# Gated product written in token order, one store per output tile, and idle products between the first groups

## The chip, the cores and the metric

The kernel runs on one core of a Trainium2 chip. The metric is the device time of one execution in microseconds. The core has a matrix engine (TensorE, in the profile PE for products and PEld for weight loads), VectorE (DVE), ScalarE (ACT), GpSimd (POOL), and SyncE (SP), which issues most of the DMA transfers. Sixteen DMA engines move the data.

## The reference

Attention over 8 batches, 12 heads, 448 tokens and head size 64, followed by a gated feed-forward layer with a product over the tokens. All inputs and the output are float32.

```python
q_n, k_n = rmsnorm(q, g_q), rmsnorm(k, g_k)
attn = softmax(q_n @ k_n.T / 8)
x = concat_heads(attn @ v)                     # 8 x 448 x 768
h = relu(x @ w_in)                             # 8 x 448 x 1024
u, v = h[..., :512], h[..., 512:]
v_n = (v - mean(v)) / sqrt(var(v) + 1e-6)
v_s = einsum('ts,bsd->btd', w_spatial, v_n) + b_spatial[None, :, None]
out = (u * v_s) @ w_out                        # 8 x 448 x 768
```

## The kernel before, in words

The order of all work is written out by hand in one string, PLAN: some 1,600 words, each of the form name.arguments/slots/engine. A word `S.3.1/12` calls `op_S` for group 3 and unit 1 with the PSUM banks 1 and 2; a last field a, v or g puts the work on ScalarE, VectorE or GpSimd. The words are run through once when the program is built, so each engine gets its instructions in the order in which its words stand, and each engine carries them out in that order. Waits between engines follow from the tiles that are read and written. PSUM is one tile `ps` of 8 banks of 512 float32 columns; the plan says which bank each result takes.

Attention goes by 24 groups (a batch and four of its heads). A group's q, k and v are loaded into `raw` (op_L, lines 287 and 292), squared (Q, L379 and L381), summed (R, L392), turned into a factor 1/rms (I and J, L405 and L410), multiplied (N, L425) and transposed, in the first groups by TensorE (P, L444, copied out by K, L362 and L463), later by a DMA transpose (T, L480). Scores are 64 x 32 products (S, L505), exponentials are taken by ScalarE (E, L513), and sums and weighted values come from TensorE again (s, a and b, L538). X (L567) divides and writes `xt`.

A token t of 448 is held as t = 7 p + c, with p below 64 and c below 7: partition p loads seven tokens that lie side by side in memory. From there on the columns of `xt` stand in the order c, p: column 64 c + p.

The second part goes by batch. V (L583, and L612 for the last 64 rows) and U (L649) multiply by the two halves of `w_in`, c and u apply the relu, B, M, m and A normalise, H (L663) is the product with `w_spT` over tokens, G (L668, VectorE) multiplies the result in PSUM by `us` and writes the gated product `gt`, and O (L677, L612 for the last rows) multiplies `gt`, as 128-column weights, by `w_out`. The 448 tokens make three tiles of 128 rows and one of 64. The copies out of PSUM (o, L360 and L362) fill `os`, and t stores it. Because the rows stand in the order c, p, a 128-row tile m holds the tokens with c = 2m in its first 64 rows and those with c = 2m + 1 in its last, and each half goes out by a transfer of its own (L701), 64 rows of 768 values that lie seven tokens apart in memory. The half tile of 64 rows goes out by L698, in the last batch in two pieces of 384 columns. All stores are issued by SyncE, as are the loads and the DMA transposes.

The words z (op_z, L252) are products of the identity with itself whose result nobody reads; they stand at the start and between the first groups. Y (L347) transposes `w_sp` by TensorE, reading its weights seven elements apart. `w_sp` lies in the space of `gt`, and so has the name gt in the profile.

Of the kernel before, what the change touches and what calls it, by code (L numbers as in the profile page):

```python
# [12 lines left out]
ALU = mybir.AluOpType  # L13
# [14 lines left out]
E.0.4/4/a P.1.0/4 R.2.1 L.6.0/2 Q.4.0/0/g E.0.3/5/a P.1.1/5 K.1.0/1/v I.2//a z.5/2 J.2//a K.1.1/1/v Q.3.0/1/a wi.1.3
N.2.1/2/v S.1.1/23 E.0.6/6/a wx//g S.1.2/45 S.1.0/67 N.2.0/3/v E.1.2/7/a L.1.2/5 P.2.1/0 E.1.0/8/a R.4.0 S.1.3/45
Q.3.1/2/g L.6.1/4 P.2.0/1 E.1.1/9/a K.2.1/2/v S.1.5/67 E.1.3/a/a R.3.0 S.1.6/23 Q.4.1/0/g Y.2/0 E.1.5/b/a K.2.0/2/v  # L30
R.3.1 E.1.6/c/a S.1.4/45 S.2.6/67 Q.5.0/1/g Y.0/1 E.2.6/d/a R.4.1 I.3//a S.2.3/23 s.0.3.1/67 J.3//a wi.1.0 s.0.1.1
E.1.4/e/a F.0//v s.0.2.1 s.0.0.1 y.0//v s.0.6.1 L.5.1/3 s.0.5.1 N.3.0/0/g E.2.3/f/a R.5.0 S.2.5/45 s.0.4.1 Y.1/1
I.4//a D.0/1/a E.2.5/g/a N.3.1/1/v L.7.1/8 P.3.0/6 D.1/0/a S.2.4/23 K.3.0/3/v L.2.2/7 S.2.1/45 F.1//g P.3.1/7
Q.6.1/2/a y.2//v y.1//v Q.6.0/0/g L.3.2/5 a.0.2.1/06 E.2.4/h/a K.3.1/3/v a.0.5.1 a.0.4.1 a.0.1.1 R.6.1 E.2.1/i/a
S.3.1/12 b.0.2.1/37 b.0.0.1 wi.0.2 b.0.6.1 E.3.1/j/a Q.5.1/1/v a.0.6.1 b.0.4.1 wi.1.2 S.3.0/45 a.0.3.1 d.0//a S.3.6/12
wi.1.1 a.0.0.1 J.4//a b.0.1.1 E.3.6/k/a N.4.1/2/v b.0.5.1 wi.0.0 b.0.3.1 E.3.0/l/a S.3.4/12 X.0.0 L.8.1/1 N.4.0/3/g
E.3.4/7/a R.5.1 S.3.3/45 E.3.3/6/a Y.3/0 X.0.1 wi.0.3 F.2//v d.1//a S.3.5/12 S.2.0/34 wi.0.1 I.5//a P.4.0/5 X.1.0
E.2.0/c/a F.3//g X.1.1 P.4.1/6 J.5//a E.3.5/e/a K.4.0/0/v N.5.1/0/g S.3.2/34 K.4.1/0/v s.2.3.1/57 E.3.2/8/a S.2.2/12
s.2.1.1 y.3//v s.2.6.1 s.2.5.1 a.2.3.1/06 E.2.2/1/a s.2.0.1 N.5.0/1/v T.5.1/0 s.2.4.1 a.2.1.1 b.2.5.1/34 Q.7.0/2/a
S.4.4/12 s.2.2.1 R.6.0 b.2.3.1 Q.7.1/1/g a.2.6.1 T.5.0/1 E.4.4/5/a b.2.0.1 a.2.0.1 b.2.1.1 R.7.0 a.2.5.1 I.6//a  # L40
a.2.4.1 D.2/1/a b.2.2.1 L.5.2/6 b.2.4.1 Q.8.1/0/g a.2.2.1 D.3/0/a R.7.1 b.2.6.1 S.4.6/12 d.2//a z.1/5 V.0.1.0/5
E.4.6/9/a L.4.2/7 X.2.0 V.0.0.0/7 L.9.1/5 X.2.1 I.7//a V.0.0.1 d.3//a L.8.0/3 Z.5/1/v V.0.1.1 J.7//a J.6//a L.9.0/9
X.3.1 S.4.1/01 N.6.1/3/g S.4.5/23 X.3.0 E.4.1/0/a V.0.1.2 V.0.2.0/4 c.0.1//v E.4.5/3/a V.0.0.2 N.7.0/2/g R.8.1
L.10.1/4 S.5.5/01 c.0.0//a S.5.4/56 S.4.2/23 E.5.5/b/a V.0.2.2 V.0.2.1 E.4.2/2/a N.6.0/0/g U.0.2.1/7 c.0.2//v P.6.1/0
E.5.4/4/a B.0.1 U.0.2.2 S.5.3/12 N.7.1/1/g B.0.0 T.6.0/3 S.5.0/34 E.5.3/a/a W.0/5 K.6.1/3/v E.5.0/f/a B.0.2 T.7.0/2
F.4//g S.5.1/01 U.0.2.0 c.0.3//v E.5.1/6/a Q.8.0/2/g U.0.0.0/6 L.6.2/0 u.0.2//v S.5.2/23 S.4.3/45 T.7.1/1 B.0.3
S.4.0/01 E.5.2/c/a U.0.1.2/7 U.0.1.0 Q.9.0/1/g E.4.3/l/a U.0.0.2 L.11.1/2 U.0.0.1 L.10.0/8 M.0//a U.0.1.1 E.4.0/i/a
u.0.0//v L.11.0/7 S.6.3/23 F.5//g S.5.6/45 R.8.0 E.6.3/j/a U.0.3.0/6 U.0.3.1 Q.9.1/0/g L.15.1/6 U.0.3.2 E.5.6/g/a
u.0.1//v S.6.6/01 u.0.3//v s.4.3.1/23 m.0//a s.4.2.1 I.8//a s.4.5.1 E.6.6/e/a R.9.0 s.4.1.1 wo b.4.0.1/45 S.6.4/67
s.4.6.1 J.8//a s.4.0.1 E.6.4/h/a A.0.0 s.4.4.1 b.4.5.1 Z.7/2/v b.4.4.1 b.4.6.1 A.0.3 D.4/1/a a.4.4.1/01 A.0.1 b.4.2.1  # L50
D.5/0/a S.7.6/67 A.0.2 b.4.1.1 a.4.6.1 E.7.6/7/a R.9.1 a.4.2.1 N.8.1/3/g a.4.1.1 b.4.3.1 a.4.0.1 d.5//a a.4.5.1
S.7.0/23 d.4//a a.4.3.1 X.5.1 H.0.2/6 I.9//a Q.11.1/2/g E.7.0/1/a X.4.1 T.8.1/0 H.0.3/5 X.5.0 J.9//a Q.11.0/1/a G.0.2
H.0.0/7 L.7.2/1 N.9.0/0/g X.4.0 F.6//a S.7.5/12 R.11.0 S.7.4/34 H.0.1/0 Q.10.1/0/a L.12.0/0 G.0.0 V.1.1.0/6 Q.10.0/1/g
L.13.0/9 E.7.5/8/a G.0.1 V.1.1.2 V.1.0.0/7 G.0.3 E.7.4/d/a V.1.1.1 R.11.1 N.8.0/2/g V.1.0.2 c.1.1//a S.6.5/01 S.7.3/23
R.10.0 S.7.2/45 E.6.5/k/a V.1.0.1 Q.15.1/2/g O.0.0.1/6 T.8.0/0 R.10.1 E.7.2/5/a O.0.2.1/0 E.7.3/4/a O.0.0.0/1 L.12.1/3
o.0.2.1/0/v N.9.1/1/g I.11//a I.10//a o.0.0.1/1/v S.6.1/23 o.0.0.0//a W.1/504 c.1.0//v E.6.1/9/a t.0.0 B.1.1 F.7//g
Q.12.0/1/a S.6.0/67 o.0.3.1/2/v S.6.2/12 T.9.1/1 V.1.2.1/3 o.0.3.0//v E.6.2/g/a O.0.1.1/4 Z.8/0/v c.1.3//v J.11//a
t.0.3 J.10//a V.1.2.0 o.0.1.1/3/a N.10.0/3/g U.1.3.0/0 R.12.0 L.8.2/5 E.6.0/2/a V.1.2.2 T.9.0/1 S.7.1/12 B.1.3
c.1.2//a S.8.0/45 S.8.5/67 N.10.1/2/g E.7.1/c/a U.1.3.1 B.1.0 L.13.1/1 U.1.0.2/3 E.8.5/0/a U.1.0.0 B.1.2 U.1.0.1
U.1.3.2 Q.12.1/0/a N.11.0/1/g T.10.1/0 O.0.2.0/1 u.1.3//a R.12.1 U.1.2.1/2 E.8.0/6/a U.1.1.1/6 L.10.2/8 U.1.2.2  # L60
L.15.0/4 Z.9/1/v M.1//a U.1.2.0 I.12//a u.1.0//v m.1//a L.14.1/7 U.1.1.2 u.1.2//a A.1.3 s.6.5.1/07 o.0.2.0//a S.9.1/34
# [93 lines left out]
def kernel(  # L155
# [18 lines left out]
    C = 7  # L174
# [566 lines left out]
```

## Time and profile before

| | |
|---|---|
| median of 3 runs | 282.5 us (281.66 to 426.04) |
| profiled execution | 280.25 us |
| its span, first to last instruction | 278.3 us |
| TensorE busy | 257.6 us, 93% of the span |
| ScalarE busy | 217.3 us, 78% |
| VectorE busy | 211.6 us, 76% |
| GpSimd busy | 128.8 us, 46% |
| moved by DMA | 55.72 MB, mean 200 GB/s |
| stores of output tiles | 55 of 192 KB and 2 of 96 KB |

The profile cuts the span into 40 slices and gives each a digit, the busy share in tenths. A row of an engine's timeline gives the start, the length, the line, the operation, the tiles, and in brackets how long the engine had been idle and what released it. A row of a group gives the busy time of all its instructions and the mean of one in ns, and then the idle time ahead of them. The row PEclk is the clock that TensorE was granted. In a row of windows the DMA share can exceed 1, because the transfers' packets overlap.

### The profile page before, as it was taken

What the parts mean: (1) busy time and instruction counts of PE and PEld (TensorE: products, weight loads), DVE (VectorE), ACT (ScalarE), POOL (GpSimd) and SP (SyncE); (2) the same over time, 40 slices, a digit from 0 to 9 for tenths busy, and PEclk for the clock granted to TensorE, in tenths of its full rate; (3) what the DMA queues carried; (4) which work ended last, traced back from release to release, by engine and by line L of the source; (5) the groups of instructions that cost most, each with busy time, mean ns of one, the idle gap of its engine ahead of it and who ended that gap; (6) DMA issues with size and microseconds to landing.
All of it is one profiled execution on the core that took longest, in us unless ns stands there. A gap on an engine that the chain in (4) does not pass through costs nothing.

```text
span 278.3 us, 10091 instructions
## 1 busy us (share of the span) xinstructions
PE 257.6 (93%) x4322; PEld 129.8 (47%) x4322; DVE 211.6 (76%) x365; ACT 217.3 (78%) x359; POOL 128.8 (46%) x99
## 2 busy tenths in 40 slices
PE   7977988988898999979999989999999999999991
PEld 3535555434354454435535443455445545555550
DVE  3899799788788787879898877798868455657740
ACT  5598799979798998599999886999999977402531
POOL 2568877896875782863779566530021100000000
PEclk9997799999999999999999999999999999999999
DMA  6999899999999999999999999395946402260446
GB/s 197 320 364 252 219 227 171 300 224 337 198 292 194 303 191 299 167 240 316 200 251 248 237 251 291 75 217 110 210 134 147 103 6 55 69 178 13 105 115 179
DMA packets 59335, 55.72 MB, mean 200 GB/s; under 512 B 35865, under 2 KB 54938, under 8 KB 59290
## 3 DMA queue, kind: packets, MB, share of 16 engines
q1 hardware_dynamic: 57778, 52.31, 78.1%
q0 software_dynamic: 1504, 2.76, 5.5%
q8 instruction: 34, 0.56, 0.9%
q14 instruction: 11, 0.09, 0.1%
q10 hardware_dynamic: 8, 0.00, 0.0%
HBM read 38.55 MB, written 11.01 MB: 178 GB/s over the span
## 4 chain that ended last, share of the span: by engine, by line
PE 59%; DMA 12%; ACT 8%; issue 6%; POOL 6%; DVE 4%; SPq 2%; POOLq 0%; ACTq 0%; DVEq 0%
PE ps L538 11%; PE ps L677 10%; PE ps L649 9%; DMA raw<-in_k_dram 8%; PE ps L505 8%; PE ps L663 8%; PE ps L583 6%; ACT et L513 6%; POOL nrm L425 4%; DMA qT<-nrm 4%; PE ps L252 3%; PE ps L612 2%; DVE ss L392 2%; DVE nrm L425 1%; POOL sqt L381 1%
## 5 line engine op out<-in xcount | busy, mean ns | idle before, releaser
L513 ACT ACTIVATE et<-ps 128x896 bf16<-128x896 f32 x168 | 146.1, 919 | 17.1 <-PE ps L505 16.1
L381 POOL TENSOR_TENSOR sqt<-raw 128x896 f32<-128x896 f32 (+1 forms) x32 | 52.8, 1654 | 29.0 <-DVE nrm L425 10.8
L505 PE MATMUL ps<-qT,kT 64*32 64x448 bf16 x1344 | 57.7, 358 | 3.7 <-DMA qT<-nrm 1.8
L425 POOL TENSOR_TENSOR nrm<-raw,rs 128x896 bf16<-128x896 f32 x30 | 50.3, 1687 | 20.2 <-ACT rs L410 10.2
L392 DVE TENSOR_REDUCE ss<-sqt 128x14 f32<-128x896 f32 x46 | 48.9, 1076 | 4.1 <-ACT sqt L379 3.5
L649 PE MATMUL ps<-xt,w_in 128*128 128x448 bf16 x192 | 43.5, 353 | 1.8 <-ACT os L360 1.8
L538 PE MATMUL ps<-et,vt 64*32 64x448 bf16 x1344 | 41.6, 349 | 2.6 <-issue 2.5
L583 PE MATMUL ps<-w_in,xt 128*128 128x512 bf16 x144 | 36.6, 380 | 0.6 <-ACT et L513 0.6
L677 PE MATMUL ps<-w_out,gt 128*128 128x384 bf16 x192 | 36.1, 326 | 0.1
L567 DVE TENSOR_TENSOR xt<-ps,rc 128x448 bf16<-128x448 f32 x48 | 27.8, 617 | 10.4 <-PE ps L538 6.6
L505 PEld LDWEIGHTS <-kT 64*32 64x32 bf16 x1344 | 19.3, 90 | 32.0 <-issue 19.9
L315 POOL CAST vt<-raw 128x896 bf16<-128x896 f32 x18 | 16.7, 930 | 34.6 <-DMA raw<-in_v_dram 28.6
L663 PE MATMUL ps<-w_spT,vn 128*128 128x448 bf16 (+1 forms) x128 | 27.3, 353 | 1.7 <-issue 1.7
L649 PEld LDWEIGHTS <-w_in 128*128 128x128 bf16 x192 | 17.5, 98 | 21.5 <-issue 7.0
L538 PEld LDWEIGHTS <-vt 64*32 64x32 bf16 x1344 | 19.9, 93 | 15.6 <-issue 4.9
L624 DVE BATCH_NORM_STATS2 s<-vs 128x6 f32<-128x512 bf16 (+1 forms) x32 | 21.7, 679 | 6.4 <-ACT vs L574 6.1
L677 PEld LDWEIGHTS <-gt 128*128 128x128 bf16 x192 | 17.9, 98 | 16.0 <-issue 3.8
L360 ACT ACTIVATE os<-ps 128x384 f32<-128x384 f32 (+1 forms) x35 | 17.2, 490 | 8.9 <-PE ps L677 8.2
L538 PE MATMUL ps<-et,ones 64*32 64x448 bf16 x672 | 23.7, 368 | 0.2 <-DVE qT L362 0.2
L362 DVE COPY os<-ps 128x384 f32<-128x384 f32 (+1 forms) x29 | 15.7, 554 | 9.3 <-PE ps L677 7.2
L668 DVE TENSOR_TENSOR gt<-ps,us 128x448 bf16<-128x448 f32 x32 | 18.9, 617 | 3.5 <-PE ps L663 2.6
L583 PEld LDWEIGHTS <-xt 128*128 128x128 bf16 x144 | 12.9, 97 | 18.0 <-issue 5.9
(62 smaller groups left out, 269.8 us busy)
## 6 DMA issues: line engine op xcount, KB each, us to landing
out_dram<-os SPq DMA_DIRECT2D x55, 192.0 KB, 3.1
raw<-in_k_dram SPq DMA_DIRECT2D x23, 448.0 KB, 6.3
raw<-in_q_dram SPq DMA_DIRECT2D x23, 448.0 KB, 7.0
raw<-in_v_dram SPq DMA_DIRECT2D x12, 448.0 KB, 5.4
raw<-in_v_dram SPq DMA_DIRECT2D x24, 224.0 KB, 5.4
w_in<-in_moe_w_in_dram POOLq DMA_DIRECT2D x8, 192.0 KB, 6.4
w_out<-in_moe_w_out_dram POOLq DMA_DIRECT2D x1, 768.0 KB, 10.8
raw<-in_k_dram SPq DMA_DIRECT2D x2, 224.0 KB, 3.3
```

The lines of the kernel that those rows point to most:

```text
L381: port(eng, eng.tensor_tensor(out=t, in0=x, in1=x, op=ALU.mult))
L392: dve.tensor_reduce(out=sss[G % 3][:, i].rearrange("p r c -> p (r c)"), in_=sqt[where.pop(("sq", G, i))].rearrange("p r (c d) -> p (r c) d ...
L425: port(eng, eng.tensor_tensor(out=nrm[sl[0]].rearrange("p c r d -> p r c d"), in0=raw[where["raw", G, i]].rearrange("p r (c d) -> p r c d" ...
L505: pe.matmul(out=ps[at:at + 32, sl[n], 0:S], lhsT=kT[64 * r:64 * r + 64, c, 64 * hh + 32 * x:64 * hh + 32 * x + 32], rhs=qT[64 * r:64 * r + ...
L513: act.activation(out=ets[sl[0]], in_=ps[:, a:b + 1:b - a, 0:S], func=AF.Exp, bias=0.0, scale=1.0)
L538: pe.matmul(out=ps[32 * l:32 * l + 32, where[kind, G][0], 0:S], lhsT=w, rhs=et_of(G, r, c)[at:at + 64], start=(n == 1), stop=(n == C), til ...
L567: dve.tensor_tensor(out=xts[b % 2][:, 2 * g + half, :], in0=ps[:, where.pop(("ab"[half], G))[0], 0:S], in1=rcs[where["rc", G]], op=ALU.mult)
L583: pe.matmul(out=ps[:, bank, :], lhsT=xts[b % 2][:, j, 128 * m:128 * m + 128], rhs=w_in[:, j % 2, j // 2, DH:], start=(n == 1 and j == 2 * ...
L624: dve.bn_stats(out=s6, in_=vss[b % SLOTS["vs"]][rows, m, :])
L649: pe.matmul(out=ps[:, bank, 0:S], lhsT=w_in[:, j % 2, j // 2, 128 * f:128 * f + 128], rhs=xts[b % 2][:, j, :], start=(n == 1 and j == 2 * ...
L663: pe.matmul(out=ps[:, sl[0], 0:S], lhsT=vns[b % SLOTS["vn"]][rows, m, 128 * f:128 * f + 128], rhs=w_spT[rows, m, :], start=(m == 0), stop= ...
L677: pe.matmul(out=ps[:, sl[0], 0:384], lhsT=gts[b % 2][:, f, 128 * m:128 * m + 128], rhs=w_out[:, f, 384 * h:384 * h + 384], start=(f == 0), ...
```

## The change

1. G writes `gt` in token order: the columns c, p of the result go to column 7 p + c. The results of VectorE so lie 7 elements of 2 bytes apart. Its two inputs are read as before.
2. The columns of `gt` that O takes as weights are now 128 tokens side by side, so each 128-row tile of the output is one block of memory. One transfer of 128 rows stores it, in place of two of 64; the half tile is the last 64 tokens.
3. Of the last batch's last half tile, the second piece is issued by ScalarE and no longer by SyncE.
4. A new word h (op_h) does n products of the identity with its first 64 columns into the 64 spare columns of bank 7. Eight of them, h.3, h.10, h.12, h.6, h.4, h.8, h.3 and h.8, 54 products in all, stand among the words of the first groups. The z words there change in size: 25, 5, 3, 4, 2, 5 and 1 become 26, 4, 4, 4, 2, 5 and 1, with the last of them at an earlier place.
5. The other words of PLAN are the same, each within 20 places of where it stood, most of them within 10 and moved by the words that are new; many take other PSUM banks.

```diff
+    def op_h(sl, e, n):
+
+        for _ in range(n):
+            pe.matmul(out=ps[:, 7, S:512], lhsT=ident, rhs=ident[:, 0:T], start=True, stop=True)
...
     def op_G(sl, e, b, f):
         assert where["us", b, f]
-        dve.tensor_tensor(out=gts[b % 2][:, f, :], in0=ps[:, where.pop(("H", b, f)), 0:S],
-                          in1=uss[b % SLOTS["us"]][:, f, :], op=ALU.mult)
+        dve.tensor_tensor(out=gts[b % 2][:, f, :].rearrange("q (p c) -> q c p", c=C),
+                          in0=ps[:, where.pop(("H", b, f)), 0:S].rearrange("q (c p) -> q c p", c=C),
+                          in1=uss[b % SLOTS["us"]][:, f, :].rearrange("q (c p) -> q c p", c=C), op=ALU.mult)
...
-    out_c = [out[b].rearrange("(p c) m -> c p m", c=C) for b in range(B)]
-
     def op_t(sl, e, b, m):
...
         if m == 3:
-            for at in sorted({tail_at(b, 0), tail_at(b, 1)}):
+            for n, at in enumerate(sorted({tail_at(b, 0), tail_at(b, 1)})):
...
-                sync.dma_start(out=out_c[b][6][:, cols], in_=t[at:at + 64, cols])
+                engines[(e or 's') if n else 's'].dma_start(out=out[b, TAIL:S, cols], in_=t[at:at + 64, cols])
             return
-        for par in range(2):
-            engines[(e or "ss")[par]].dma_start(out=out_c[b][2 * m + par], in_=t[64 * par:64 * par + 64])
+        engines[e or "s"].dma_start(out=out[b, 128 * m:128 * m + 128, :], in_=t)
```

More of the change, by code (lines that the diff above doesn't have):

```diff
@@ L28 @@
[L28 to L37, printed above, removed]
@@ L143 @@
[L143 to L147 removed]
+l.1.0/0 setup l.0.0/1 l.0.1 z.26/0 gl.1//a l.1.1 gl.0//a L.1.1/2 L.1.0/3 L.2.0/4 q.1.0/0/a L.2.1/5 r.1.0 L.4.0/6 wb/0
@@ new lines @@
+S.2.1/34 L.2.2/7 F.1//g P.3.1/6 y.2//v Q.6.1/2/a y.1//v Q.6.0/0/g L.3.2/5 a.0.2.1/25 K.3.1/3/v a.0.5.1 a.0.4.1
+E.2.4/h/a a.0.1.1 R.6.1 S.3.1/67 E.2.1/i/a b.0.2.1/01 wi.0.2 b.0.0.1 b.0.6.1 Q.5.1/1/v a.0.6.1 E.3.1/j/a wi.1.2
+b.0.4.1 S.3.0/34 a.0.3.1 wi.1.1 d.0//a S.3.6/67 a.0.0.1 wi.0.0 J.4//a b.0.1.1 E.3.6/k/a N.4.1/2/v b.0.5.1 b.0.3.1
+E.3.0/l/a S.3.4/67 X.0.0 L.8.1/1 N.4.0/3/g E.3.4/7/a R.5.1 S.3.3/34 Y.3/2 E.3.3/6/a X.0.1 wi.0.3 S.3.5/67 F.2//v
+d.1//a S.2.0/34 wi.0.1 P.4.0/0 I.5//a X.1.0 E.2.0/c/a F.3//g X.1.1 P.4.1/5 J.5//a E.3.5/e/a K.4.0/0/v N.5.1/0/g
@@ new lines @@
+S.16.2/34 b.14.1.1 b.14.0.1 E.16.2/j/a S.17.2/12 X.14.1 V.4.2.1/5 E.17.2/7/a V.4.2.0 Q.22.0/2/g R.20.0 T.19.0/3
+V.4.2.2 I.21//a S.17.3/67 R.22.1 c.4.2//a S.17.1/12 U.4.3.2/3 E.17.3/g/a F.19//g U.4.3.1 X.15.1 V.4.1.0/4 E.17.1/e/a
+Z.18/3/v U.4.3.0 R.22.0 V.4.1.2 Q.23.0/0/g u.4.3//a V.4.1.1 Q.20.1/1/a S.16.1/01 S.18.5/23 W.4/756 E.18.5/c/a R.20.1
+E.16.1/l/a c.4.1//v V.4.0.1/2 o.3.3.0/3/a o.3.3.1//v V.4.0.2 c.4.3//a B.4.1 S.18.4/01 t.3.3 S.17.4/34 J.21//a
+S.16.4/56 E.18.4/k/a N.21.1/2/g T.19.1/0 V.4.0.0 B.4.2 U.4.1.0/7 E.17.4/1/a U.4.1.1 c.4.0//v U.4.1.2 I.20//a
@@ new lines @@
+N.21.0/0/g B.4.0 E.16.4/3/a S.17.5/01 T.21.1/1 S.18.0/23 O.2.1.0/4 B.4.3 E.18.0/9/a O.3.2.1/5 Q.23.1/2/g u.4.1//v
+M.4//a T.21.0/1 U.4.2.1/6 I.22//a m.4//a o.2.1.0//v J.20//a U.4.2.0 E.17.5/i/a U.4.2.2 t.2.1 S.17.6/23 u.4.2//v
+s.16.4.1/47 s.16.5.1 E.17.6/5/a L.22.2/2 S.18.3/01 A.4.1 s.16.1.1 s.16.0.1 A.4.0 L.18.2/0 s.16.2.1 E.18.3/6/a
+o.3.2.1/1/v s.16.3.1 S.18.6/23 s.16.6.1 Z.19/2/v S.18.1/56 E.18.6/f/a A.4.2 U.4.0.0/0 A.4.3 U.4.0.1 N.20.0/1/v
+D.16/0/a U.4.0.2 J.22//a H.4.3/1 D.17/1/a N.20.1/3/v u.4.0//a T.20.0/0 H.4.2/7 E.18.1/0/a G.4.3 H.4.0/0 d.17//a
@@ L148 @@
+O.6.0.1/2 t.6.2 M.7//a m.7//a o.6.0.0/0/a U.7.2.0/3 A.7.2 o.6.3.1//a U.7.1.1/4 A.7.3 o.6.0.1//a A.7.1 U.7.1.2 t.6.3
+A.7.0 U.7.1.0 U.7.2.1 t.6.0 u.7.1//a U.7.2.2 H.7.2/0 u.7.2//v u.7.0//v H.7.0/1 H.7.3/2 G.7.0 H.7.1/3 G.7.3 G.7.2
+O.6.1.0/1 G.7.1 O.6.1.1/0 o.6.1.0/1/a O.7.1.0/2 o.6.1.1//a O.7.1.1/1 t.6.1 o.7.1.0/3/a O.7.0.1/0 o.7.1.1//a O.7.0.0/2
+t.7.1 o.7.0.1/4/v O.7.2.0/1 o.7.0.0//a O.7.2.1/0 t.7.0 o.7.2.0/2/v W.8/23 o.7.2.1//a t.7.2 o.7.3.0/0/v o.7.3.1//a
+t.7.3//a
 """
```

220 lines of the change are left out of this document (105 added, 115 removed).

## The prediction

> **What bounds the kernel now.** I read the page's busy shares first, then the windows by stage, the TensorE timeline, and last the chain of waits and the SyncE queue.
>
> ```profile
> PE 257.6 (93%) x4322; PEld 129.8 (47%) x4322; DVE 211.6 (76%) x365; ACT 217.3 (78%) x359; POOL 128.8 (46%) x99
> ...
> PEclk9997799999999999999999999999999999999999
> DMA  6999899999999999999999999395946402260446
> ```
> ```profile
> 16.00:25.00 9.00, 5.95 (x106) 3.69 (x97) 8.51 (x10) 8.97 (x14) 6.55 (x6) 1.00 1.08 339
> 25.00:31.80 6.80, 6.80 (x120) 3.86 (x119) 5.82 (x8) 4.58 (x9) 5.48 (x5) 0.50 0.77 183
> 31.80:34.00 2.20, 2.12 (x46) 1.52 (x51) 1.08 (x3) 2.20 (x4) 2.20 (x2) 1.00 0.94 275
> ...
> 80.00:180.00 100.00, 94.57 (x1742) 45.42 (x1738) 83.27 (x142) 88.31 (x147) 63.59 (x44) 1.00 1.06 236
> 175.00:272.00 97.00, 96.41 (x1425) 49.49 (x1421) 67.23 (x128) 67.04 (x115) 8.77 (x8) 1.00 0.47 111
> ```
>
> The columns are the length, the busy time of PE, PEld, DVE, ACT and POOL, the granted clock, the DMA share and GB/s. The reader is to see four stages. From 16 to 25 us VectorE and ScalarE are full and TensorE is idle for 9.00 - 5.95 = 3.05 us. From 25.0 to 31.8 the clock stands at 0.50 and TensorE, full, holds the others up. Up to 180 the DMA engines are full too (share 1.06), with TensorE idle 5.4 us in 100. From 175 to 272 TensorE is idle 0.6 us in 97: only shorter TensorE work could help there. After that comes a tail of stores.
>
> The largest TensorE gap of the middle stage, and the chain behind it:
>
> ```profile
> 117.57 0.55 PE L649 MATMUL ps<-xt,w_in 128*128 128x448 bf16 x2
> 119.95 0.92 PE L649 MATMUL ps<-xt,w_in 128*128 128x448 bf16 x4 [1.83 <-ACT os L360]
> ```
> ```profile
> 101.60 0.61 SPq L480
> ...
> 102.26 0.58 SPq L701
> ...
> 102.89 0.59 SPq L701
> ...
> 104.23 0.48 SPq L701
> ...
> 104.75 0.62 SPq L701
> ...
> 108.40 10.07 DMA raw<-in_k_dram
> ```
>
> SyncE issues without pause from 101.6 to 108.4, four half-tile stores among it; a key load issued behind them takes 10.07 us and lands at 118.47. ScalarE's square starts 0.1 us later:
>
> ```profile
> 118.57 0.95 ACT L379 ACTIVATE sqt<-raw 128x896 f32<-128x896 f32 x1 [2.62 <-POOL vt L315]
> 119.43 0.47 ACT L360 ACTIVATE os<-ps 128x384 f32<-128x384 f32 x1
> ```
>
> The row puts its wait down to GpSimd's cast; the chain, which looks at the load, fits the time better. The output copy behind the square holds a PSUM bank that TensorE wants.
>
> **The change, part by part.**
>
> *Idle products.* Eight groups, 54 products of 64 columns with a 128-column weight load each, are added to TensorE between about 15 and 25 us; the larger idle products (z) become one more in all. The nearest price is that of the 128-column transposes:
>
> ```profile
> L444 PE MATMUL ps<-ident,nrm 128*128 128x128 bf16 x70 | 5.5, 220 | 1.8 <-ACT et L513 1.0 <-DVE nrm L425 0.6 <-DVE xt L567 0.2
> ```
> ```profile
> 17.29 1.01 PE L444 MATMUL ps<-ident,nrm 128*128 128x128 bf16 x14 [0.71 <-ACT et L513]
> ...
> 19.98 0.76 PE L505 MATMUL ps<-qT,kT 64*32 64x448 bf16 x24 [0.73 <-DVE kT L463]
> ```
>
> Fourteen take 1.01 us, 0.072 us each. So 54 x 0.072 = 3.9 us, against the 3.05 us of idle time: nearly all is covered by gaps. Not all: in the built program the group of ten begins only when the exponential ahead of the transposes has ended, and the group of twelve only when the key copy on VectorE has, which is where TensorE starts again anyway (0.71 and 0.73 us above). Those two run behind the gap, not in it: 10 x 0.072 = 0.72 before the transposes, covered because VectorE comes to the copy of the transposed tile late, and 12 x 0.072 = 0.86 before three score units. ScalarE has one exponential (0.92 us) to spend there. I charge 0.4; ends 0 and 1.6.
>
> *Clock.* What this buys: the drop began at 25.0 after TensorE had worked 5.95 of 9 us, much of it transposes. If it goes, the stretch of 6.80 us is worth at most half, 3.4 us (0.50 against 1.00), by TensorE alone. But the others must follow: VectorE was idle only 6.80 - 5.82 = 0.98 us in it, and 2.20 - 1.08 = 1.12 in the 2.2 us behind, which it waited for the same products: 2.1 in all. Between 0.98 and 2.1 I take 1.5. Late next is VectorE. Ends: 0 (the clock drops anyway) and 2.1. [...]
>
> *Stores.* 48 stores of 64 rows on SyncE become 24 of 128 rows; bytes stay the same. Each issue takes 0.48 to 0.62 us above, so two of the four in the chain go, 2 x 0.57 = 1.1 us. The load behind is issued that much earlier, but its 10.07 us are full DMA engines, and where these stay full it lands no earlier. The gap is 1.83: ends 0 and 1.83, and I take 0.9. The stores themselves, and the loads they are compared with:
>
> ```profile
> 18.00:19.00 1.00, 1.00 (x11) 0.53 (x8) 0.97 (x2) 1.00 (x3) 1.00 (x1) 1.00 1.06 385
> ```
> ```profile
> 270.00:272.00 2.00, 2.00 (x18) 1.05 (x16) 0.73 (x2) 0.88 (x2) 0.00 (x0) 1.00 0.93 253
> ...
> 274.00:276.00 2.00, 0.00 (x0) 0.00 (x0) 0.00 (x0) 0.00 (x0) 0.00 (x0) 1.00 0.90 257
> ```
>
> Per full engine the half-tile stores reach 257/0.90 = 286 GB/s, loads over 128 partitions 385/1.06 = 363. If a 128-row store moves like such a load, 393 KB take 1.08 us for 1.37.
>
> *Tail.*
>
> ```profile
> 270.78 3.31 SPq L701 DMA_DIRECT2D out_dram<-os  x4
> ...
> 272.39 0.55 DVE L362 COPY os<-ps 64x384 f32<-64x384 f32 x1 [0.92 <-PE ps L612]
> 274.19 1.19 SPq L698 DMA_DIRECT2D out_dram<-os  x2
> ```
>
> The last copy ends at 272.94, but SyncE, four stores behind, issues the last two only from 274.19 to 275.38. With two issues fewer and ScalarE taking the second half tile, both leave at 272.95: the second began at about 274.8, so up to 1.85 us. The bytes set the other end: at 257 GB/s the engines are full nearly to the end, so as little as 0.3. I take 1.2. On ScalarE nothing is queued behind that issue.
>
> *Gated product.* VectorE now writes its 448 results 14 bytes apart, in 32 instructions. No row shows such a write.
>
> ```profile
> L668 DVE TENSOR_TENSOR gt<-ps,us 128x448 bf16<-128x448 f32 x32 | 18.9, 617 | 3.5 <-PE ps L663 2.6
> ...
> L425 DVE TENSOR_TENSOR nrm<-raw,rs 128x896 bf16<-128x896 f32 x16 | 18.0, 1135 | 2.5 <-POOL nrm L425 1.8 <-POOL vt L315 0.3 <-ACT rs L410 0.2
> ...
> L381 DVE TENSOR_TENSOR sqt<-raw 128x896 f32<-128x896 f32 x3 | 3.3, 1085 | 1.4 <-DMA raw<-in_k_dram 1.4
> ...
> L612 PEld LDWEIGHTS <-gt 128*64 128x64 bf16 x64 | 5.9, 109 | 1.2 <-issue 0.3
> ...
> L347 PEld LDWEIGHTS <-gt 64*64 64x64 bf16 x49 | 4.3, 193 | 2.0 <-issue 2.0
> ```
>
> Below: 0, no faster, since the same elements stream from PSUM. On the same engine the normalisation writes its output permuted in runs of 64 and takes 1135 against the square's 1085 ns: +50. Above: the weight load L347 reads 64 columns 14 bytes apart in 193 ns, L612 64 side by side in 109, a factor 1.77: 617 would become 1092, +475 each. I take +0.05 us, from the row on VectorE, and keep 0.475 for the range. At the end four of these stand in a row ahead of the last output products:
>
> ```profile
> 265.61 1.69 DVE L668 TENSOR_TENSOR gt<-ps,us 128x448 bf16<-128x448 f32 x3
> ...
> 266.10 5.43 PE L677 MATMUL ps<-w_out,gt 128*128 128x384 bf16 x32
> ```
>
> The last ends at 267.30; eight products of the previous batch cover it, 266.26 to 267.56 (5.27 us for 32, 0.163 each). The cover is 0.26 us, so 4 x 0.05 costs nothing.
>
> *Moved words and banks.* The order of the rest shifts by a few places and other PSUM banks are drawn. One such bank wait is 0.7 us (17.29 above); I take 0, ends -0.7 and +0.7.
>
> **Sum.** 1.5 + 0.9 + 1.2 - 0.4 = 3.2 us. The profiled execution took 280.25 (span 278.3), the median of the runs is 282.5, 2.25 more. So 277.05 against its own, and 282.5 - 3.2 = 279.3 for a median. Its own range is 277.1 (clock 2.1, gap 1.83, tail 1.85) to 281.6 (0.98, 0 and 0.3).
>
> **The rivals.**
>
> *Everything adds up.* Clock 2.1, gap at 118 wholly 1.83, tail 1.85, and the VectorE and ScalarE wait of 0.7 at the banks, less nothing, with 0.6 from faster stores (two tiles in the tail, 0.29 each): 7.1, so 275.4. For it: all these are on the chain. Against it: DMA share 1.06 in the middle stage takes gains back.
>
> *It does not do what it says.* The clock drops all the same, or the early gain is absorbed by the full DMA engines; only the tail is left, less the idle products: 1.2 - 0.4 = 0.8, so 281.7. For it: share 1.06 from 80 to 180. Against it: the DMA share fell to 0.77 in the slow stretch, so the loads had waited for the engines.
>
> *The product written apart becomes the bound.* Place: L668, VectorE. With d more each, the end loses 4d - 0.26. Of the 28 earlier ones I let half show, since VectorE is idle 16.7 us in 80 to 180: 14d. At 18d - 0.26 = 3.2, d = 0.19, the change gains nothing; at d = 0.5 it is 2% slower; at the upper row's 0.475 it is 8.3 - 3.2 = 5.1 slower, 287.6, and 294.2 if all 28 show (32d - 0.26 = 14.9). For it: L347. Against it: L347 is a read on another engine, and its excess of 84 ns over 64 columns is 1.3 ns a column, little over the 617/448 = 1.38 that VectorE takes anyway. [...]
>
> **How the numbers follow.** Forecast 0.48, all gains 0.2, little left 0.17, slower product 0.15. Two per cent, about what a measurement of this kernel can tell from no change, is 5.65 us: below 276.85 is faster, above 288.15 slower. All gains count as faster, 0.2. Of the slow product two thirds, 0.1, count as slower: those with more than half of it showing, or dearer than the upper row. The forecast, "little left" and the other third are same, 0.7. The range reaches from 275.4, all gains, to 284.0, where d is 0.27 by 18d - 0.26 - 3.2 = 1.5, and leaves out most of the slow product (0.13) and some 0.05 below.
>
> **What would show it.** Clock right: a granted clock of 1.00 between 25 and 32, with TensorE work after it earlier by 1 to 2 us. Stores right: some 33 stores instead of 57 and a gap at L649 near 118 below 1.8 us. Tail right: last copy to end under 4.5 us (5.4 now). Product right: its mean at 617 to 670 ns. Wrong: a mean above 800 ns, new waits of TensorE on it, or a clock that falls elsewhere.

## The result and the profile after

The changed kernel takes 316.81 us (median of 4 runs, 316.17 to 317.67) against 282.08 beside it: a ratio of 1.1247 with an interval of 1.1194 to 1.1299. The forecast was 279.3 with a range up to 284.0; the change costs 34.7 us, more than the rival of the slower product gave even with every product showing (294.2). The profiled execution took 316.17 us, span 314.2.

The page of the changed kernel, its busy times, its granted clock, four groups of instructions and its stores:

```profile
PE 270.0 (86%) x4361; PEld 135.9 (43%) x4377; DVE 247.6 (79%) x365; ACT 219.8 (70%) x359; POOL 129.0 (41%) x99
...
PEclk9999979997999989999999999999999979999989
...
L511 PE MATMUL ps<-qT,kT 64*32 64x448 bf16 x1344 | 60.5, 359 | 11.7 <-DVE gt L674 8.2
...
L674 DVE TENSOR_TENSOR gt<-ps,us 128x448 bf16<-128x448 f32 x32 | 58.5, 1992 | 2.4 <-PE ps L669 2.0
...
L544 PE MATMUL ps<-et,vt 64*32 64x448 bf16 x1344 | 45.4, 367 | 11.6 <-DVE gt L674 6.5
...
L684 PE MATMUL ps<-w_out,gt 128*128 128x384 bf16 x192 | 39.3, 345 | 4.0 <-DVE gt L674 4.0
...
out_dram<-os SPq DMA_DIRECT2D x24, 384.0 KB, 2.5
...
out_dram<-os SPq DMA_DIRECT2D x7, 192.0 KB, 2.9
```

One line explains most. The gated product, now L674, has a mean of 1992 ns where L668 had 617, and its busy time goes from 18.9 to 58.5 us. (32 times 1375 would be 44.0; the busy time grows by 39.6, 1.24 each, since the records of neighbouring instructions overlap: the means add up to 63.7 us where the busy time is 58.5, and before to 19.7 where it was 18.9.) TensorE's idle time is 314.2 - 270.0 = 44.2 us, against 20.7 before. The view of that one line tells for whom VectorE was late:

```profile
  PE ps L511: 8.2, 8
  PE ps L544: 6.5, 7
  PE ps L684: 4.0, 3
  PE ps L618: 2.2, 2
  PE ps L589: 1.7, 2
  PEld L618: 1.6, 1
  PE ps L669: 1.3, 2
  PEld L684: 1.2, 1
  PE ps L655: 1.1, 1
```

The first number is the wait in us, the second how often. The rows of PE add up to 25.0 us, close to the 23.5 by which TensorE's idle time grew. Most of it is not the output product that reads `gt`: it is attention (L511, L544), which does not read `gt` at all. Its results go into PSUM banks that hold a result of H until the gated product has read it. In PLAN the scores S.8.2/56 stand four words behind G.1.0, whose input lies in bank 5, and the values b.6.3.1/34 ten words behind G.1.2, whose input lies in bank 3. Both wait in the second batch:

```profile
107.27 0.38 PE L511 MATMUL ps<-qT,kT 64*32 64x448 bf16 x8 [1.90 <-DVE gt L674]
...
109.03 2.07 PE L544 MATMUL ps<-et,vt 64*32 64x448 bf16 x40 [0.62 <-DVE gt L674]
```

Of the signs that the prediction named, those of the other parts came out as it said: 33 stores instead of 57; the clock stays up from 25 to 32 us (1.00, where it was 0.50 from 25.0 to 31.8); the last copy ends 3.8 us before the end, not 5.4. They hardly matter beside 39.6 us of VectorE. All three signs of being wrong came too: a mean above 800 ns, TensorE's waits on the product, and a clock that falls elsewhere (first at about 41 us, to 0.50 up to 44, and to 0.51 near the end).

In what follows medians are over all runs of a kernel, while ratios leave out runs more than 1.5% above the fastest of their kernel; the kernel before spread from 275 to 287 us in these sets, so that where a median and a ratio disagree by a per cent, nothing is concluded from one of them alone.

### The profile page after: what moved, and what is told of

Its sections match the earlier page's. It is cut to its first block, busy times and chain, and to the rows that moved or that the text cites. A ratio compares the mean times of both kernels' runs of the same rounds, so it can differ in the third digit from the quotient of the medians.

```text
span 314.2 us, 10142 instructions
## 1 busy us (share of the span) xinstructions
PE 270.0 (86%) x4361; PEld 135.9 (43%) x4377; DVE 247.6 (79%) x365; ACT 219.8 (70%) x359; POOL 129.0 (41%) x99
## 5 line engine op out<-in xcount | busy, mean ns | idle before, releaser
L511 PE MATMUL ps<-qT,kT 64*32 64x448 bf16 x1344 | 60.5, 359 | 11.7 <-DVE gt L674 8.2
L674 DVE TENSOR_TENSOR gt<-ps,us 128x448 bf16<-128x448 f32 x32 | 58.5, 1992 | 2.4 <-PE ps L669 2.0
L544 PE MATMUL ps<-et,vt 64*32 64x448 bf16 x1344 | 45.4, 367 | 11.6 <-DVE gt L674 6.5
L684 PE MATMUL ps<-w_out,gt 128*128 128x384 bf16 x192 | 39.3, 345 | 4.0 <-DVE gt L674 4.0
L511 PEld LDWEIGHTS <-kT 64*32 64x32 bf16 x1344 | 20.9, 91 | 42.2 <-issue 35.5
L589 PE MATMUL ps<-w_in,xt 128*128 128x512 bf16 x128 | 34.5, 384 | 3.2 <-DVE gt L674 1.7
L544 PEld LDWEIGHTS <-vt 64*32 64x32 bf16 x1344 | 22.0, 95 | 26.1 <-issue 17.9
L366 ACT ACTIVATE os<-ps 128x384 f32<-128x384 f32 (+1 forms) x35 | 17.2, 491 | 20.2 <-PE ps L684 19.5
L684 PEld LDWEIGHTS <-gt 128*128 128x128 bf16 x192 | 18.6, 102 | 22.1 <-issue 10.3
L544 PE MATMUL ps<-et,ones 64*32 64x448 bf16 x672 | 23.2, 356 | 0.0
L589 PEld LDWEIGHTS <-xt 128*128 128x128 bf16 x144 | 12.9, 99 | 19.5 <-issue 8.0
```

What stands on the lines that cost most here:

```text
L511: pe.matmul(out=ps[at:at + 32, sl[n], 0:S], lhsT=kT[64 * r:64 * r + 64, c, 64 * hh + 32 * x:64 * hh + 32 * x + 32], rhs=qT[64 * r:64 * r + ...
L544: pe.matmul(out=ps[32 * l:32 * l + 32, where[kind, G][0], 0:S], lhsT=w, rhs=et_of(G, r, c)[at:at + 64], start=(n == 1), stop=(n == C), til ...
L589: pe.matmul(out=ps[:, bank, :], lhsT=xts[b % 2][:, j, 128 * m:128 * m + 128], rhs=w_in[:, j % 2, j // 2, DH:], start=(n == 1 and j == 2 * ...
L674: dve.tensor_tensor(out=gts[b % 2][:, f, :].rearrange("q (p c) -> q c p", c=C), in0=ps[:, where.pop(("H", b, f)), 0:S].rearrange("q (c p) ...
L684: pe.matmul(out=ps[:, sl[0], 0:384], lhsT=gts[b % 2][:, f, 128 * m:128 * m + 128], rhs=w_out[:, f, 384 * h:384 * h + 384], start=(f == 0), ...
```

## Experiments: is it the product?

**The change without the step, and the step without the change.** One kernel is the changed one with the product's result side by side again (the rows of the output then come in another order). The other is the kernel before with only its product changed.

```diff
  e1_plain_product: the changed kernel, but
-        dve.tensor_tensor(out=gts[b % 2][:, f, :].rearrange("q (p c) -> q c p", c=C),
+        dve.tensor_tensor(out=gts[b % 2][:, f, :],
  e2_strided_only: the kernel before, but
-        dve.tensor_tensor(out=gts[b % 2][:, f, :],
+        dve.tensor_tensor(out=gts[b % 2][:, f, :].rearrange("q (p c) -> q c p", c=C),
```

> The changed kernel with one thing undone: the gated product is written side by side again, as before the change; the one store per tile stays, so the rows of the output stand in another order. Theory A (the slowdown is all the product's, 1.99 us for 0.62, 32 times): 277 to 282 us, the sum of the other steps as predicted, 279.3. Theory B (the other steps, idle products, banks and stores, lose time themselves): over 285 us, with TensorE waits that do not name the product.

> The kernel before with one thing of the change: the product's results 14 bytes apart; stores and plan as before, so the rows of the output stand in another order. Theory A: 314 to 322 us, the whole loss, a mean of the product near 1990 ns. Theory B: well under 310 us. If half of the 32 x 1.37 = 44 us showed, as the prediction's rival took it, 282 + 22 + 3 = 307.

The first took 283.47 us against 283.46 beside it (ratio 1.0122, 1.0035 to 1.0210), the second 314.49 (1.1167, 1.1027 to 1.1308). The product makes nearly all of the loss: without its step the change is even by the medians and 1.2% slower by the ratio, and the step alone brings 31 of the 35 us. The group's rows on the two pages:

```profile
L674 DVE TENSOR_TENSOR gt<-ps,us 128x448 bf16<-128x448 f32 x32 | 19.0, 618 | 3.7 <-PE ps L669 2.7
```
```profile
L668 DVE TENSOR_TENSOR gt<-ps,us 128x448 bf16<-128x448 f32 x32 | 58.4, 1991 | 5.0 <-PE ps L663 4.6
```

## Experiments: what in the product?

**Read at a step instead of written at a step.** The same permutation can be made on the reading side: results side by side, PSUM read at a step of 64 elements of 4 bytes and `us` at 64 of 2.

```diff
-        dve.tensor_tensor(out=gts[b % 2][:, f, :].rearrange("q (p c) -> q c p", c=C),
-                          in0=ps[:, where.pop(("H", b, f)), 0:S].rearrange("q (c p) -> q c p", c=C),
-                          in1=uss[b % SLOTS["us"]][:, f, :].rearrange("q (c p) -> q c p", c=C), op=ALU.mult)
+        dve.tensor_tensor(out=gts[b % 2][:, f, :].rearrange("q (p c) -> q p c", c=C),
+                          in0=ps[:, where.pop(("H", b, f)), 0:S].rearrange("q (c p) -> q p c", c=C),
+                          in1=uss[b % SLOTS["us"]][:, f, :].rearrange("q (c p) -> q p c", c=C), op=ALU.mult)
```

> The changed kernel with the product's loops the other way round: results written side by side, token by token, and both inputs read at steps (256 bytes in PSUM, 128 in SBUF); the output is complete. Theory C (it is the write at a step that costs): the product near 620 ns and 277 to 282 us. Theory D (every access at a step costs, reads too): the product at 1.5 us or more and over 305 us.

It took 287.24 us (1.0294, 1.0194 to 1.0394). Its group:

```profile
L674 DVE TENSOR_TENSOR gt<-ps,us 128x448 bf16<-128x448 f32 x32 | 28.7, 936 | 3.4 <-PE ps L669 3.0
```

The mean is 936 ns, half as long again as 618, where the write at a step has 1992. The time lies between the two theories, nearer to C: reading at a step is cheap here, though not free.

**Each access by itself.** A kernel without the computation runs each form four times from the same tiles, one behind the other on its engine.

```diff
+            dve.tensor_tensor(out=y16, in0=p_, in1=u_, op=mult)                    # L740
+            dve.tensor_tensor(out=perm(y16), in0=two(p_), in1=two(u_), op=mult)    # L742, 14 bytes
+            dve.tensor_tensor(out=cols(x16, n), in0=p_, in1=u_, op=mult)           # L748 to L754, n = 2, 4, 8, 16 elements
+            dve.tensor_tensor(out=cols(x32, 8), in0=p_, in1=u_, op=mult)           # L758, float32
```

> No attention at all: four runs each of the product of 448 results on VectorE with results 2, 4, 8, 14, 16 and 32 bytes apart, in bfloat16 and float32, with reads at steps, the same copy on ScalarE and VectorE, and TensorE products with a moving operand read at a step. The output is zeros. [...] Half-word theory (what costs is a write of 2 bytes that does not join its neighbour): already 4 bytes near 2000, and float32 at any step near 620.

The groups by line; the last number ahead of the second bar is the mean of one in ns:

```profile
L752 DVE TENSOR_TENSOR x<-ps,us 128x448 bf16<-128x448 f32 x4 | 8.6, 2138 | 0.1
L754 DVE TENSOR_TENSOR x<-ps,us 128x448 bf16<-128x448 f32 x4 | 8.1, 2025 | 0.1
L762 ACT ACTIVATE y<-ps 128x448 bf16<-128x448 f32 x4 | 7.6, 1898 | 0.1
L742 DVE TENSOR_TENSOR y<-ps,us 128x448 bf16<-128x448 f32 x4 | 7.5, 1887 | 0.1
...
L750 DVE TENSOR_TENSOR x<-ps,us 128x448 bf16<-128x448 f32 x4 | 4.6, 1149 | 0.1
...
L756 DVE TENSOR_TENSOR y<-ps,us 128x448 f32<-128x448 f32 x4 | 4.0, 1005 | 0.1
L758 DVE TENSOR_TENSOR x<-ps,us 128x448 f32<-128x448 f32 x4 | 3.8, 958 | 0.1
L744 DVE TENSOR_TENSOR y<-ps,us 128x448 bf16<-128x448 f32 x4 | 3.6, 901 | 0.1
...
L748 DVE TENSOR_TENSOR x<-ps,us 128x448 bf16<-128x448 f32 x4 | 2.6, 655 | 0.1
L740 DVE TENSOR_TENSOR y<-ps,us 128x448 bf16<-128x448 f32 x4 | 2.5, 624 | 4.3 <-PE ps L253 4.2
L746 DVE TENSOR_TENSOR y<-ps,us 128x448 bf16<-128x448 f32 x4 | 2.5, 624 | 0.1
...
L760 ACT ACTIVATE y<-ps 128x448 bf16<-128x448 f32 x4 | 2.2, 543 | 65.5 <-DVE x L758 65.4
L764 ACT ACTIVATE y<-ps 128x448 bf16<-128x448 f32 x4 | 2.2, 543 | 0.1
```

Two-byte results 2, 4, 8, 14, 16 and 32 bytes apart take 624, 655, 1149, 1887, 2138 and 2025 ns. Beyond 16 bytes the time grows no further (2025 at 32), and below it falls with the step, so the results can be counted by stretches of 16 bytes, called lines in an expectation below. At 16 bytes every result has a stretch of its own, at 14 bytes eight results lie in seven, at 8 bytes two lie in one: 7/8 of 2138 is 1871 (measured 1887), half of it 1069 (1149). So in these rows the price of two-byte results goes by the stretches written, 2138/448 = 4.8 ns each; where four results share one (655) or eight (624) it hardly shows, while two in one (the 8-byte step) still take 1149 for 624. The half-word theory fails: at 4 bytes no result joins its neighbour, and 655 is nearly free. Float32 results, each in a stretch of its own, cost half (958 and 1005, where the theory wanted 620). So a stretch has no one price; it depends on the size of the result, and why it does stays open. ScalarE pays the same for its copy at 14 bytes, 1898 against 543. Reading PSUM at a step alone is free on both engines (L746, 624 as L740, and L764, 543 as L760); what made 936 of 618 in the kernel above is `us`, read at a step from SBUF (L744, 901, against L746, 624).

## Experiments: how much of it shows?

**More VectorE time without a step.** The kernel before, with every product computed twice into the same place.

```diff
+        h = where.pop(("H", b, f))
+        for _ in range(2):
+            dve.tensor_tensor(out=gts[b % 2][:, f, :], in0=ps[:, h, 0:S], ...)
```

> The kernel before with each gated product computed twice, side by side, into the same place: 0.62 us more VectorE time per product, between the 0.32 of the reads at a step and the 1.375 of the writes at a step. If VectorE's time alone counts and each batch hides about 1 to 1.3 us of its four products, 32 x 0.62 - 8 x 1.15 = 10.6: 289 to 294 beside the kernel before at 281.5. If the write at a step disturbs others beyond VectorE's time (the lines of SBUF), plain double time costs far less: 283 to 286.

```profile
L670 DVE TENSOR_TENSOR gt<-ps,us 128x448 bf16<-128x448 f32 x64 | 38.4, 620 | 3.8 <-PE ps L663 2.3
```

It took 292.24 us against 280.52 (1.0388, 1.0330 to 1.0446). Of 38.4 - 18.9 = 19.5 us added, 11.7 show and 7.8 are hidden: 1.0 us per batch. The product read at a step added 28.7 - 19.0 = 9.7 busy and cost 3.8 beside the plain one: 5.9 hidden, 0.7 per batch. The changed kernel added 39.6 and, beside its mended form below (0.6 us above its own kernel before, where the changed one is 34.7 above), costs 34.1: 5.5 hidden, 0.7 per batch. By three sizes and two kinds, a batch hides 0.7 to 1.0 us of its four products on average, and the rest shows; each of the three differences is uncertain by about 2 to 4 us, so by 0.2 to 0.5 per batch. Nothing beyond VectorE's time, and the waits it causes, is needed to explain the loss.

The average is not a rule for each batch. Where the first gated product of each batch starts in this kernel's profile, less where it starts in the kernel before, is -0.1, 1.5, 1.6, 4.7, 4.8, 6.9, 8.1 and 9.8 us, and the end is 12.5 later. Each batch adds 2.4 us of VectorE. From the second batch to the third and from the fourth to the fifth no lateness is added, from the third to the fourth and from the last to the end at least all of it. So how much is hidden goes with the place. The waits above make it likely that what counts is how soon TensorE wants the banks that the products hold, but these runs do not show it batch by batch.

**The last batch alone.** The kernel before, with the step in the last four products only.

```diff
+        if b == 7:
+            dve.tensor_tensor(out=gts[b % 2][:, f, :].rearrange("q (p c) -> q c p", c=C), ...)
```

> The kernel before with the product at a step in the last batch alone (4 of 32 products, the rows of the last batch's output come in another order). Theory 1, each batch has its own slack and the last batch has little of it: 4 x 1.375 = 5.5 us more VectorE time, of which 3.2 (what the last batch added in the changed kernel, +31.4 to +34.6) to 5.2 us show, so 285 to 287 beside the kernel before at 282. Theory 2, the loss is one of sustained VectorE load only, and four products by themselves are caught up: within 1 us of the kernel before. If 5.2 or more shows, the last batch has no slack at all, and the other seven batches hid all that was hidden.

It took 287.56 us against 281.55 (1.0331, 1.0219 to 1.0444), 6 us for four products by the medians and more by the ratio. In the profiles it is 5.6: from the first of the four to the end 19.1 us pass instead of 13.5. So the last batch hides nothing, and whatever is hidden is hidden in the other seven. Its timeline of VectorE and TensorE at the end, and then the windows there:

```profile
263.91 7.10 DVE L669 TENSOR_TENSOR gt<-ps,us 128x448 bf16<-128x448 f32 x4 [0.42 <-PE ps L663]
```
```profile
265.86 0.81 PE L682 MATMUL ps<-w_out,gt 128*128 128x384 bf16 x4 [0.52 <-DVE gt L669]
269.32 7.68 PE L682 MATMUL ps<-w_out,gt 128*128 128x384 bf16 x28 [2.66 <-DVE gt L669]
```
```profile
266.00:268.00 2.00, 0.67 (x4) 0.29 (x3) 2.00 (x2) 0.49 (x1) 0.00 (x0) 1.00 0.00 0
268.00:270.00 2.00, 0.68 (x3) 0.34 (x3) 2.00 (x2) 0.00 (x0) 0.00 (x0) 0.60 0.00 0
270.00:272.00 2.00, 2.00 (x7) 0.65 (x6) 1.01 (x1) 0.49 (x1) 0.00 (x0) 0.50 0.02 4
272.00:274.00 2.00, 2.00 (x8) 0.98 (x7) 0.00 (x0) 0.96 (x2) 0.00 (x0) 0.50 0.75 195
```

The four products take 7.10 us where 18.9/8 = 2.36 was their share: 4.74 more. TensorE works a third of the time from 266 to 270, its granted clock (the number behind the five engines) falls to 0.50, and the 28 products from 269.32 on take 7.68 us where 32 took 5.43. A late engine is paid twice here, once in the wait and once in the clock behind it. The changed kernel has the same at its end: 0.51 from 303.4 to 306.9. With the product done twice TensorE waited 1.57 us in that place and the clock stayed at 1.00.

## Experiments: the other parts of the change

**Token order without the step.** The permutation can be put where the single accesses show it free (624 and 543 ns, as without it): the relu copies of `u` read PSUM at a step and write `us` in token order, and the product reads PSUM at a step. Both write side by side.

```diff
-        relu(engines[e], uss[b % SLOTS["us"]][:, f, :], ps[:, where.pop(("U", b, f))[0], 0:S])
+        relu(engines[e], uss[b % SLOTS["us"]][:, f, :].rearrange("q (p c) -> q p c", c=C),
+             ps[:, where.pop(("U", b, f))[0], 0:S].rearrange("q (c p) -> q p c", c=C))
...
+        dve.tensor_tensor(out=gts[b % 2][:, f, :].rearrange("q (p c) -> q p c", c=C),
+                          in0=ps[:, where.pop(("H", b, f)), 0:S].rearrange("q (c p) -> q p c", c=C),
+                          in1=uss[b % SLOTS["us"]][:, f, :].rearrange("q (p c) -> q p c", c=C), op=ALU.mult)
```

> The changed kernel with the product mended: the relu copy of u reads PSUM at a step and writes us in token order, and the product reads PSUM at a step and us side by side, so that no write and no SBUF read is at a step; the output is complete. If reads of PSUM at a step cost nothing, as in the step measurement, the product takes 0.62 us and the time is that of the changed kernel with the plain product, within 1% of the kernel before. If the relu copy pays for the step on either engine, 32 x 0.3 us more work, near the 287 us of the other loop order.

It took 282.02 us against 281.39 (1.0061, 1.0020 to 1.0101), and its product 617 ns. With that mend the parts can be told apart, all against the same 281.39:

- the new order, banks and idle products with the product and the stores of before (e6_order_only)
- the mended kernel without its 54 idle products (e7_no_idle: `range(n)` becomes `range(0)` in op_h)
- PLAN of before with the mended product, single stores and the last half tile on ScalarE (e5_stores_only)

> The new order, banks and idle products, with the product and the stores of the kernel before. Theory P: 1 to 2.5 us slower than the kernel before, TensorE behind by 2 us or more from 60 us on. Theory Q: within 0.5 us of it. If the clock alone had been worth the predicted 1.5 us: faster by 1.

> The mended changed kernel without its 54 new idle products. [...] If they cost more than they bring, it is faster by up to 1.5 us.

> The order of work and the banks of the kernel before, no new idle products; only token order by way of the mended product, one store per tile and the last half tile on ScalarE. Theory P (stores gain, the new order and idle products lose about as much): 1 to 2.5 us under the kernel before, most of it in the tail. Theory Q (the stores are hidden by the full DMA engines and the tail is bound by bytes): within 0.5 us of it.

They took 286.57 (1.0188, 1.0123 to 1.0253), 281.88 (1.0020, 0.9979 to 1.0061) and 279.08 us (0.9955, 0.9920 to 0.9991). The last is faster than both kernels, if only by 0.1 to 0.8% of the kernel before. Between it and the one without idle products lies the new order alone: 2.8 us against it by the medians, 1.8 by the ratios. The first, which has the new order and the idle products and none of the gains, lost 5.2 us, more than either theory said; in its profile the exponentials run 4 to 6 us behind those of the kernel before from 108 us on. Where the new order loses is to be seen in part in the windows of e7_no_idle, first, and e5_stores_only:

```profile
190.00:240.00 50.00, 48.67 (x940) 24.21 (x932) 31.86 (x59) 42.22 (x63) 3.67 (x4) 1.00 0.38 98
```
```profile
190.00:240.00 50.00, 50.00 (x1014) 25.40 (x999) 32.79 (x61) 41.74 (x65) 3.67 (x4) 1.00 0.41 102
```

In the stage where TensorE is the bound it now idles 1.33 us, in two places where the score products wait 0.6 us each for an exponential; the rest has no row that I could find.

**Idle products.** With them the mended kernel takes 282.02, without 281.88 (by the ratios 0.4% apart). In the old order they were put at the same places, once as often and once three times:

```diff
  e9_idle_old_order: e5_stores_only, with the words h.3 to h.8 put into its PLAN
  e13_idle_three: the same, with
-        for _ in range(n):
+        for _ in range(3 * n):
```

> The old order and banks with the mended token order, one store per tile and the last half tile on ScalarE (279.08 without idle products), plus the 54 idle products at the places where the changed kernel has them. Theory 1, what the clock gives early is absorbed by about 127 us where loads set the pace: 278.6 to 279.6, no change, while the clock's first drop moves from 26 to about 41 us. Rival, the early clock is worth 1.5 to 3 us at the end and was eaten by the new order in the other runs: 276 to 277.6. Rival, the idle products cost the order: 280 or more.

> As the kernel with idle products in the old order (281.22) but three times as many, 162 for 54: 108 x 0.072 = 7.8 us more TensorE work between 15 and 40 us. If the middle stage takes up early offsets of 3 to 4.5 us (as two kernels showed), 3 to 5 us of it are left: 284 to 286. If it takes up everything early, no change: 280 to 282. If nothing is taken up: 289.

They took 281.22 us against 281.55 (1.0061, 0.9988 to 1.0133) and 280.02 against 280.52 (0.9875, 0.9785 to 0.9965). The granted clock by slices of e5_stores_only and of e9_idle_old_order:

```profile
PEclk9999587999899999999999999999999999999998
```
```profile
PEclk9999797999999999999999999999999999999999
```

Neither 54 nor 162 of them, 7.8 us more of TensorE by the row of the prediction, move the end by as much as the runs spread, and by the medians neither kernel is faster for having them. The two rows of the clock differ as hoped, though with the 54 its first drop still comes at 29 us and not at 41. But other profiles of the old order without idle products differ as much: from 20 to 50 us the mean granted clock was 0.89 with 54 and with 162, and 0.77 to 0.94 in the eight profiles without (the kernel before among them). In the new order it was 0.94 in all five profiles that have them and 0.72 in e7_no_idle. On the face of it the rival came nearer, that they cost the old order: 281.22 stands 2.3 us above e10_tail_sync below (by the ratios 0.4%), which lies beside it without them and with the last half tile on SyncE. But three times as many cost no more than that, so this is not settled.

Two pairs of traces show how an early difference goes: set against the kernel before, the exponentials (L513) of e5_stores_only are 4.5 us late at 76 to 85 us, 1.1 at 127 and 0.0 from 181 on. The mended kernel is 2.9 us ahead of e7_no_idle at 44 us and has 0.3 of it left at 190. So the stage between takes up a gain as well as a loss; that full DMA engines do it is argued from the DMA share of 1.06 there, not shown. It does not always happen: e9_idle_old_order is 2.8 us late at 83 and 2.7 us late from 190 on.

**Stores.** From e5_stores_only: the last half tile back on SyncE, and each tile sent by two or by four stores of consecutive tokens.

```diff
  e10_tail_sync: t.7.3//a becomes t.7.3
  e11_two_stores: e5_stores_only, and
  e12_four_stores: e10_tail_sync, with (64 and 32 rows)
-        engines[e or "s"].dma_start(out=out[b, 128 * m:128 * m + 128, :], in_=t)
+        for at in range(0, 128, 32):
+            engines[e or "s"].dma_start(out=out[b, 128 * m + at:128 * m + at + 32, :], in_=t[at:at + 32])
```

> As the 279.08 kernel (old order, mended token order, one store per tile) but the last half tile stored by SyncE. If the 2.3 us of that kernel come from the last half tile's own queue, this one gives them back: 280.3 to 281.5. If they come from single stores, it stays within 0.5 us: 278.6 to 279.6.

> As the 279.08 kernel but with each output tile sent by two stores of 64 rows of consecutive tokens instead of one of 128. If halving the stores is worth what is gained, it goes back by 0.9 to 2 us: 280 to 281. If only the tail matters, it stays within 0.5 us of 279.1. If the kind of rows matters (consecutive rows against rows of every seventh token), it also stays, since the rows here are consecutive.

> As the 278.91 kernel (old order, mended token order, last half tile on SyncE) but with each output tile sent by four stores of 32 rows, all on SyncE, 96 instead of 24. If the number of store issues on SyncE is what cost the kernel before its 2 to 2.6 us (24 issues more there), 72 issues more cost at least twice that: 284 to 288. If SyncE's issues are covered, it stays at 279 to 281.

They took 278.91 against 281.55 (1.0022, 0.9968 to 1.0076), 281.86 against the same (1.0115, 1.0016 to 1.0214) and 285.42 against 280.52 (1.0145, 1.0096 to 1.0193). By both measures more stores are slower, and which engine issues the last piece makes no difference that could be told. Against the kernel before, though, one store per tile wins 2.3 and 2.6 us by the medians (e5 and e10), 1.3 and nothing by the ratios. The SyncE queue at the end, of e10_tail_sync and then of e12_four_stores:

```profile
262.96 10.16 SPq L705 DMA_DIRECT2D out_dram<-os  x5
273.35 1.11 SPq L703 DMA_DIRECT2D out_dram<-os  x2
```
```profile
264.28 14.26 SPq L706 DMA_DIRECT2D out_dram<-os  x20
278.64 1.11 SPq L703 DMA_DIRECT2D out_dram<-os  x2
```

In the first the last copy ends at 273.32 and its store is issued at once, 4.1 us before the end. In the second the copy ends at 274.55, but SyncE is still at its twenty issues and reaches the last pieces 4.1 us later, and 7.9 us pass from copy to end. The kernel before and e11_two_stores, with ten issues there, need 5.4 and 5.2; over all profiles it is 4.4 to 6.0 with ten (six of them) and 3.5 to 4.9 with five (nine). So about 1 us in the tail is right, and the number of issues brings it, though single profiles of the two kinds overlap. The rest of the gain in the medians, 1 us or more, has no place in the profiles that holds from run to run.

## Why the prediction was wrong

- *Gated product: wrong, and this decided.* The step that failed is "I take +0.05 us, from the row on VectorE, and keep 0.475 for the range". It measured 1.375 us, nearly three times the upper end. The nearer row wrote its results permuted too, but in runs of 64 side by side (128 bytes); the other row was a read by TensorE. Neither was the thing that costs: a write of two-byte results 14 bytes apart, which took 1887 ns by itself where side by side took 624. I gave the rival of the slower product 0.15 because no row showed such a write, and bounded the price by rows that did not contain it.
- *Half of the 28 earlier products shows: wrong.* It came from an average idle share of VectorE. What was hidden came to 0.7 to 1.0 us per batch on average, and four products at 1.24 us of busy time each are far past that: 5.5 of 39.6 us were hidden in all. Most of the waits are for PSUM banks that the products hold, a path that the sum did not follow except in the last batch. With the measured price the formula 18d - 0.26 gives 24.5 and a time near 304, so price and showing both fell short of 316.8.
- *The end loses 4d - 0.26: right in kind, short in size.* With the measured price it gives 5.2; four products cost 4.74 us of VectorE and some 6 in all: behind the wait the granted clock was 0.50, and 28 output products took 7.68 us where 32 had taken 5.43.
- *Clock, 1.5: the sign came in the new order, its worth was wrong.* That the added products would hold the clock was my assumption; no row of before shows it. In the changed kernel the drop at 25 us did go (1.00 from 25 to 32 us), from 20 to 50 us the mean clock in the new order was 0.94 with them and 0.72 without, and the mended kernel had gained 2.9 us by 44 us; all but 0.3 of them were gone by 190. This was the rival "the early gain is absorbed", for this term alone. In the old order no effect of the same products on the clock can be told.
- *Stores, 0.9, and tail, 1.2: about right by the medians, too high by the ratios.* 2.3 us together in e5_stores_only (2.1 forecast), 1.3 by the ratio. The tail came from fewer issues on SyncE and not from ScalarE's queue. The gap of 1.83 at L649 is gone in e10_tail_sync, but the work ahead of it came later by nearly as much.
- *Idle products, 0.4 against: between 0 and 2.3 by these runs, not to be told from 0.*
- *Moved words and banks, 0 with ends of 0.7: wrong.* They cost 2.8 us by the medians and 1.8 by the ratios, in part in a stage that I had called bound by TensorE and then left out when I asked what a new order could cost.

The parts so named give 281.4 - 2.3 + 2.8 + 0.1 = 282.0, the time of the mended kernel, but only because each was read off beside the next. The one run that could test the sum does not fit it: the new order and the idle products together, 2.9 us by these parts, cost 5.2 in e6_order_only. What is shown is that without the step the change is within about 2% of the kernel before, and that of its parts only the stores won anything, by the medians.

## What to carry to other kernels

Put a permutation on the side that reads PSUM, and write side by side; two-byte results 14 or 16 bytes apart made the VectorE instruction here 3.0 and 3.4 times as long (1887 and 2138 ns against 624), and at 14 bytes the ScalarE copy 3.5 times (1898 against 543). When the trace has no row for a new access, find the row that shares its feature (here: how far apart the results are written), and if there is none, do not let the nearest rows close the range. Hidden time is counted per place in the order, by what waits there next (here the PSUM bank that a product holds), and not as a share of an engine's idle time.

## What the runs showed of the hardware

- Two-byte results written to SBUF 32, 16 and 8 bytes apart took VectorE 2025, 2138 and 1149 ns for 448 of them: 4.5, 4.8 and 5.1 ns for each stretch of 16 bytes written (448, 448 and 224). At 14 bytes (392 stretches) VectorE and ScalarE alike took 4.8 (1887 and 1898 ns). Float32 results 32 bytes apart took 958 ns, 2.1 each.
- Reading PSUM at a step of 256 bytes costs VectorE and ScalarE nothing (624 and 543 ns, as side by side), while reading two-byte `us` from SBUF at 128 bytes took 901 for 624.
- TensorE pays for a moving operand read at a 128-byte step: 24 products of 448 columns took 18.3 us instead of 6.4 (L774 and L772 of the kernel of single accesses), 0.76 us each instead of 0.27.
- In the changed kernel TensorE was busy 1.79 of 5.4 us from 298.0 to 303.4, at a granted clock of 1.00, and the clock was 0.51 from 303.4 to 306.9. In the kernel with the step in the last batch it was busy 1.35 of 4 us from 266 to 270, and the clock was about 0.50 for 6.8 us (268.4 to 275.2, worked out from the windows' means of 0.60, 0.50, 0.50 and 0.69). Both are close to the end.
